# A new order for the prologue of a fused attention and MLP kernel on one core

## The chip, the cores and the metric

The kernel runs on one core of one Trainium2 chip. The metric is the device time of one execution in microseconds (us). Executions of one and the same kernel spread here by more than the effect under study: the kernel before took between 1108.5 and 1114.3 us in the rounds below. So small differences are read in two ways: from times taken in alternating rounds on one chip, with a 95% interval, and from the trace of one execution of each kernel, which shows where in that run each microsecond was spent. e1 to e4 ran on one chip, e5 to e8 on a second, e9 to e12 on a third.

PE is the matmul engine and PEld its weight loads, DVE the vector engine, ACT the scalar engine, POOL the general engine, and SP the engine that issues most DMAs (483 of the 485 in the profile before).

## The reference, cut to what matters

```python
x  = A_x                                  # 2048 tokens x 1024, bf16
xn = layernorm(x)
s  = attention(xn, wqkv, wo)              # 32 heads of 32
g  = silu(gelu(layernorm(xn) @ w1 + b1) @ w2 + b2)      # 3584 hidden
return x + s * g
```

The token tiles (16 tiles of 128 tokens) must be normed and transposed before anything else can run.

## The kernel before

A small list scheduler in the kernel's Python fixes the order of instructions on every engine. The program lets engines wait for each other only by semaphores. The run is cut into "units": a unit has the scores of two key tiles for one group of four heads (`s_unit`, PE), their exp (`exp_unit`, two ACT instructions) and the product with V (`pv_unit`, PE). There are 512 units. Units 0 to 7 are the prologue, which also norms and transposes the tokens and makes K, Q and V of the first heads. From unit 8 on, PE does one "dense" item in each unit (an MLP or projection piece), as the string `PLAN` lists them; that is over 1,000 us of the run.

```python
def norm_pair(p):                        # two token tiles at a time
    more = p + 1 < NP
    if more and p >= 2: stat(2 * p + 2)  # bn_stats, bn_aggr on DVE
    nbias(p)
    xnorm(2 * p); xnorm(2 * p + 1)       # DVE, into one of 4 buffers
    if more:
        if p < 2: stat(2 * p + 2)
        stat(2 * p + 3)
        rstd(p + 1)                      # DVE add, POOL pow
    ycoef(p)                             # POOL

stat(0); stat(1); rstd(0); norm_pair(0); transp_pair(0)

def pro_unit(p):
    if p + 1 < NP: norm_pair(p + 1)
    if p < 3: ynorm(p)
    if 0 < p < NP - 1: transp_pair(p + 1)    # PE transposes, ACT copies to xnT
    pair_kq(p)                               # K and Q: 64 matmuls; two ACT copies
    pair_v(p)                                # V: 64 matmuls; one ACT copy
    if p == 0: transp_pair(1)
# ...
while u < NU + LAG or ...:
    if u < NP: pro_unit(u)
    if u == 4: load_y(0)
    if 4 <= u < NP: load_sub(0, u - 4)       # first MLP weights, 256 KB each
    s_unit(u); exp_unit(u); pv_unit(u - 1)
    if u >= NP: ...                          # one dense item of PLAN
```

The biases `b1` and `b2` are loaded at the start by POOL, as two DMAs of single elements (4,640 packets for 0.02 MB on the page).

The softmax here doesn't subtract the row's maximum and nothing guards it: scores larger than these inputs give would overflow.

Of the kernel before, what the change touches and what calls it, by code (L numbers as in the profile page):

```python
# [13 lines left out]
a v a a a q a q a v a v a a a q a a v a q a a v q a a v a a q a q a a v q a q a a a q q v a a q w3 w4 w3 w4 v w4 w2 w2 w2 a a v a q v v a q q a a a a a q a q a a q a a v a q a q q a a a v v a a a q v a a a a q q a a w3 v w3 w4 w4 w4 q v q v w2 v q w3 w3 a a a v v q a a a q a a q q a a a q q a v a q a v a a q a q a a a a v a a q a q v v v a a q q q v a q q a w3 q v q w5 q w4 w3 q w3 w4 w2 w4 a a a v v a a q a a q a q q v a a q a q v a q a a a a q a a a q a a v a a a a v a v a q a v q q w3 w4 v q w4 w4 w4 v w4 w3 w4 a a a q q a a a a v a v a a a a a v q a a v a a a q a a a v a a q q v a q q a a q a q q q a v w3 v w4 w4 q w4 w4 w4 w4 w4 a a a a q q a a q a a q a a a q a q q a a a a a a a a a a q q a a a a a q a q w2 w4 w3 w4 w2 w3 w5 o o o o o o o o o o o o w4 o o o o o o o o o o o o o o o o o o o o o o o o o o o . o o o o o o o . o o  # L14
# [153 lines left out]
def bass_recurrent_scan__mha_block__mixer_channel_mlp__prompt_kernel(  # L168
# [42 lines left out]
    with ExitStack() as st:  # L211
# [42 lines left out]
        xnb = [hflat[:, i * D:(i + 1) * D] for i in range(4)]  # L254
# [28 lines left out]
        for tb in range(4):  # L283
            load_x(tb)
            if tb in (1, 3):
                load_wq(0, (1 if tb == 1 else 0,))
        load_x(4)
        load_x(5)
        load_wq(0, (2,))
        for tb in range(6, NT):  # L290
            load_x(tb)
# [4 lines left out]
        op("gpsimd", lambda e: e.dma_start(b1T[:], B_b1.rearrange("(fb p) -> p fb", p=128)), w=["b1"], dma="b1", c=256)  # L296
        op("gpsimd", lambda e: e.dma_start(b2h[:], B_b2.rearrange("(nb p) -> p nb", p=128)), w=["b2"], dma="b2", c=64)

# [9 lines left out]
        def rstd(b):  # L308
            lo, hi = 2 * b, 2 * b + 2
            L = lambda k: lnp[:, k, lo:hi]  # L310
            mvk = [("mv", t) for t in range(lo, hi)]
            op("vector", lambda e: e.tensor_scalar_add(L(0), mv[:, lo:hi, 1], EPS), r=mvk, w=[("l0", b)], c=169.0)
            op("gpsimd", lambda e: e.tensor_tensor(L(2), L(0), mhalf[:, 0:2], op=ALU.pow), r=[("l0", b), "mhalf"], w=[("l2", b)], c=708.0)  # L313

        def nbias(b):
            lo, hi = 2 * b, 2 * b + 2
            L = lambda k: lnp[:, k, lo:hi]
            mvk = [("mv", t) for t in range(lo, hi)]
            op("vector", lambda e: e.scalar_tensor_tensor(L(3), mv[:, lo:hi, 0], -1.0, L(2), op0=ALU.mult, op1=ALU.mult),
               r=mvk + [("l2", b)], w=[("l3", b)], c=107.0)  # L320

        def ycoef(b):
            lo, hi = 2 * b, 2 * b + 2
            L = lambda k: lnp[:, k, lo:hi]
            mvk = [("mv", t) for t in range(lo, hi)]
            op("gpsimd", lambda e: e.tensor_tensor(L(4), mv[:, lo:hi, 1], L(2), op=ALU.mult), r=mvk + [("l2", b)], w=[("l4", b)])
            op("gpsimd", lambda e: e.tensor_tensor(L(4), L(4), L(2), op=ALU.mult), r=[("l4", b), ("l2", b)], w=[("l4", b)])
            op("gpsimd", lambda e: e.tensor_scalar(L(4), L(4), 1.0, EPS, op0=ALU.mult, op1=ALU.add), r=[("l4", b)], w=[("l4", b)])
            op("gpsimd", lambda e: e.tensor_tensor(L(5), L(4), mhalf[:, 0:2], op=ALU.pow), r=[("l4", b), "mhalf"], w=[("l5", b)], c=760.0)
            op("gpsimd", lambda e: e.tensor_tensor(L(6), L(2), L(5), op=ALU.mult), r=[("l5", b), ("l2", b)], w=[("l6", b)])  # L330
            op("gpsimd", lambda e: e.tensor_tensor(L(7), L(3), L(5), op=ALU.mult), r=[("l5", b), ("l3", b)], w=[("l7", b)])

        def xnorm(tb):
            i = tb % 4
            op("vector", lambda e: e.tensor_scalar(xnb[i], xst[:, tb * D:(tb + 1) * D], lnp[:, 2, tb:tb + 1], lnp[:, 3, tb:tb + 1],  # L335
                                                   op0=ALU.mult, op1=ALU.add),
               r=[("xst", tb), ("l2", tb // 2), ("l3", tb // 2)], w=[("xnb", i)], c=545.0)
# [7 lines left out]
        pro_banks = [4, 5, 7]  # L345
        pbk = {"n": 0}
# [5 lines left out]
        def transp(tb):  # L352
            i, bk = tb % 4, pro_bank()
# [129 lines left out]
        def w1_item(c, f):  # L483
# [14 lines left out]
            def fin(bk):  # L498
# [30 lines left out]
                def gate(i, xq, kq, fq):  # L529
                    op("vector", lambda e: e.scalar_tensor_tensor(hT[:, fq, 0:n], ut[:, i, 0:n], 1.0, xq[:, 0:n], op0=ALU.add, op1=ALU.mult),  # L530
                       r=[kus[i], kq], w=[("hT", fq)] + ([("xnb", i) for i in range(4)] if c == 0 else []), c=151 + 1.042 * n)
                    busy.difference_update((kq, kus[i]))
                    have.add((c, fq))
# [92 lines left out]
        def pair_kq(p):  # L626
            t0, bk = 256 * p, pro_bank()

            def f(e):
                for which, off in ((1, 0), (0, 256)):  # L630
# [3 lines left out]
                return ins  # L634
            op("tensor", f, r=[("wq", 0), ("wq", 1), ("xnT", 2 * p), ("xnT", 2 * p + 1)], w=[("b", bk)], c=("col", 16, 256))
            for nm, dst, off in (("KT", KT, 0), ("QT", QT, 256)):
                op("scalar", lambda e, dst=dst, off=off: e.activation(dst[0][:, t0:t0 + 256], bank(bk, off, off + 256), ACT.Copy),
                   r=[("b", bk)], w=[(nm, 0, 2 * p), (nm, 0, 2 * p + 1)], c=263.0)
# [14 lines left out]

        def norm_pair(p):

            more = p + 1 < NP
            if more and p >= 2:
                stat(2 * p + 2)
            nbias(p)
            xnorm(2 * p)  # L660
            xnorm(2 * p + 1)
            if more:
                if p < 2:
                    stat(2 * p + 2)
                stat(2 * p + 3)
                rstd(p + 1)
            ycoef(p)

        def transp_pair(p):
            transp(2 * p)  # L670
            transp(2 * p + 1)

        stat(0)
        stat(1)
        rstd(0)
        norm_pair(0)
        transp_pair(0)

        def pro_unit(p):
            if p + 1 < NP:  # L680
                norm_pair(p + 1)
            if p < 3:
                ynorm(p)
            if 0 < p < NP - 1:
                transp_pair(p + 1)
            pair_kq(p)
            pair_v(p)
            if p == 0:
                transp_pair(1)


# [12 lines left out]
        DU = NP  # L704
# [136 lines left out]
        while u < NU + LAG or state["qi"] < total or dq or act_tasks:  # L841
# [5 lines left out]
            if u == 4:  # L847
                load_y(0)
            if 4 <= u < NP:
                load_sub(0, u - 4)  # L850
# [3 lines left out]
            if u < NU:  # L854
                exp_unit(u)
            if LAG <= u < NP:
                pv_unit(u - LAG)
            if u >= NP and state["qi"] < total:
                qi = state["qi"]
                entry = flat[qi]  # L860
                state["qi"] += 1
                if entry:
                    it, lo, hi = entry
                    for hp, which in loads.pop(qi, ()):
                        if hp < HG // 2:
                            load_wq(hp, which)
# [77 lines left out]
```

## Time and profile before

| | before |
|---|---|
| time, median of the first 3 runs | 1110.45 us |
| span of the profiled run | 1108.7 us |
| first transpose on PE | 8.15 us |
| scores of unit 1, 3, 8 start | 24.87, 35.84, 59.28 us |

The start of the scores of unit 8 is the hand-over from the prologue to the dense part.

The windows view of the kernel before gives each engine's busy time in stretches of the run; the first column is the stretch and the second its length.

```profile
core 0: us, PE busy (x) PEld busy (x) DVE busy (x) ACT busy (x) POOL busy (x), PEclk, DMA share, GB/s
0.00:25.00 25.00, 13.95 (x320) 10.87 (x320) 19.64 (x49) 10.59 (x15) 11.89 (x30) 1.00 1.13 254
25.00:57.00 32.00, 32.00 (x1000) 27.23 (x992) 14.88 (x39) 27.36 (x41) 12.10 (x34) 1.00 0.27 68
60.00:1050.00 990.00, 980.41 (x27104) 631.53 (x27100) 559.00 (x1250) 968.12 (x1098) 0.00 (x0) 1.00 0.40 115
```

PE is idle for 11 us of the first 25 and for nothing from 25 to 57. In the dense part PE and ACT are both nearly full.

The chain of waits of the kernel before, in order of time (start, us, what):

```profile
19.18 1.08 PE ps L357 x16
20.26 1.26 PE ps L366 x37
21.52 0.62 issue
22.14 2.79 PE ps L366 x91
24.93 0.33 PE ps L761 x8
...
56.79 0.60 ACT VP L651
57.39 1.84 ACT P L773 x2
59.23 0.05 issue
59.28 0.40 PE ps L761 x8
```

L357 are the transposes, L366 all projections, L761 the scores.

The DMA view of the kernel before over the first 14 us (packets, MB, share of the 16 engines):

```profile
q1 hardware_dynamic: 3787, 3.05, 83.3%
q0 software_dynamic: 3659, 0.01, 40.6%
```

The second line is the biases.

### The profile page before, as it was taken

To read this page: it belongs to the slowest core of one execution; us is meant where nothing else is said; L and a number is where in the kernel's file an instruction comes from. 1 tells how busy PE (TensorE), PEld (TensorE's weight loads), DVE (VectorE), ACT (ScalarE), POOL (GpSimd) and SP (SyncE) were. 2 spreads that over 40 slices of the span, in tenths; PEclk is the share of its full clock that TensorE was granted. 3 is DMA by queue.
4 is the path that set the end of the run, shared out by engine and by line. 5 is a ranking of instruction groups with operands and counts; after the bars stand their busy time and mean duration, and the time that the engine had idled before them with its cause. 6 is when DMAs were issued, how large, how long until landed. Compare 5 with 4: busy or idle time off the path is not lost.

```text
span 1108.7 us, 63340 instructions
## 1 busy us (share of the span) xinstructions
PE 1082.7 (98%) x29952; PEld 706.5 (64%) x29952; DVE 630.4 (57%) x1415; ACT 1049.5 (95%) x1197; POOL 24.0 (2%) x64
## 2 busy tenths in 40 slices
PE   6999999999999999999999999999999999999998
PEld 4866666666666666666666666666666666666665
DVE  8468762377742477652276852277743377624556
ACT  4899999899999999999999999999999999999994
POOL 4300000000000000000000000000000000000000
PEclk9999999999999999999999999999999999999999
DMA  9245255323353323333433334433234324557353
GB/s 237 71 145 174 89 146 153 114 79 108 99 150 98 89 80 114 110 87 88 130 108 92 115 76 126 144 111 108 80 104 118 111 81 144 159 155 156 96 136 108
DMA packets 202420, 129.93 MB, mean 117 GB/s; under 512 B 45488, under 2 KB 192944, under 8 KB 202160
## 3 DMA queue, kind: packets, MB, share of 16 engines
q1 hardware_dynamic: 197520, 125.86, 39.7%
q8 instruction: 234, 3.83, 1.4%
q0 software_dynamic: 4640, 0.02, 0.6%
q14 instruction: 26, 0.21, 0.1%
HBM read 104.87 MB, written 12.58 MB: 106 GB/s over the span
## 4 chain that ended last, share of the span: by engine, by line
PE 65%; ACT 32%; DVE 2%; issue 1%; DMA 0%; POOL 0%
PE ps L366 41%; ACT P L773 29%; PE ps L761 10%; PE ps L790 7%; PE ps L793 7%; ACT u L524 3%; DVE stats L303 1%; PE ps L357 1%; ACT thz L566 0%; DMA OT<-in_A_x_dram 0%; DVE hT L335 0%; DVE wq L614 0%; POOL lnp L313 0%; DVE mv L305 0%; DVE xb L507 0%
## 5 line engine op out<-in xcount | busy, mean ns | idle before, releaser
L773 ACT ACTIVATE P<-ps 128x1024 bf16<-128x1024 f32 x1024 | 970.0, 1069 | 18.1 <-PE ps L761 11.9
L793 PE MATMUL ps<-P,ones 128*32 128x256 bf16 x4096 | 257.7, 273 | 0.6 <-issue 0.5
L790 PE MATMUL ps<-P,VP 128*32 128x256 bf16 x4096 | 257.5, 273 | 0.0
L366 PE MATMUL ps<-hT,war 128*32 128x352 bf16 (+1 forms) x5376 | 226.1, 309 | 1.5 <-issue 1.4
L366 PE MATMUL ps<-yTc,war 128*32 128x352 bf16 (+1 forms) x5376 | 226.4, 309 | 0.4 <-issue 0.4
L761 PE MATMUL ps<-QT,KT 32*128 32x256 bf16 x4096 | 204.1, 273 | 7.6 <-ACT P L773 5.5
L366 PEld LDWEIGHTS ps<-hT,war 128*32 128x32 bf16 x5376 | 128.0, 96 | 76.2 <-issue 27.6
L366 PEld LDWEIGHTS ps<-yTc,war 128*32 128x32 bf16 x5376 | 127.5, 96 | 75.8 <-DVE xb L507 17.2
L562 DVE TENSOR_SCALAR zh<-ps,b2h 128x352 f32<-128x352 f32 (+1 forms) x48 | 27.5, 573 | 207.4 <-PE ps L366 207.4
L507 DVE TENSOR_SCALAR xb<-ps,b1T 128x352 f32<-128x352 f32 (+1 forms) x168 | 96.2, 573 | 78.5 <-PE ps L366 75.3
L761 PEld LDWEIGHTS ps<-QT,KT 32*128 32x128 bf16 x4096 | 61.0, 92 | 119.8 <-issue 65.7
L366 PE MATMUL ps<-xnT,wq 128*32 128x352 bf16 (+2 forms) x3200 | 130.0, 306 | 2.1 <-DMA wq<-in_A_wqkv_dram 1.5
L790 PEld LDWEIGHTS ps<-P,VP 128*32 128x32 bf16 x4096 | 110.4, 97 | 21.4 <-issue 1.7
L793 PEld LDWEIGHTS ps<-P,ones 128*32 128x32 bf16 x4096 | 110.5, 97 | 19.6 <-issue 1.1
L530 DVE SCALAR_TENSOR_TENSOR hT<-u,xb 128x352 bf16<-128x352 f32 (+1 forms) x168 | 83.8, 508 | 62.3 <-ACT u L524 62.2
L366 PEld LDWEIGHTS ps<-xnT,wq 128*32 128x32 bf16 x3200 | 77.5, 97 | 41.6 <-DVE xb L507 10.7
L517 DVE SCALAR_TENSOR_TENSOR u<-u,xb 128x352 f32<-128x352 f32 (+1 forms) x168 | 82.5, 509 | 1.9
L513 DVE TENSOR_TENSOR u<-xb 128x352 f32<-128x352 f32 (+1 forms) x168 | 82.5, 508 | 0.8
L524 ACT ACTIVATE u<-u 128x704 f32<-128x704 f32 (+1 forms) x84 | 69.9, 833 | 0.0
L366 PE MATMUL ps<-wq,xnT 128*32 128x256 bf16 x2048 | 66.6, 274 | 1.8 <-issue 1.1
L366 PE MATMUL ps<-xnT,OT 128*32 128x352 bf16 (+1 forms) x1536 | 62.9, 309 | 0.2 <-DVE wq L614 0.2
L366 PEld LDWEIGHTS ps<-wq,xnT 128*32 128x32 bf16 x2048 | 50.2, 96 | 14.0 <-DVE xb L507 5.5
(44 smaller groups left out, 435.5 us busy)
## 6 DMA issues: line engine op xcount, KB each, us to landing
war<-in_B_w_dram SPq DMA_DIRECT2D x336, 256.0 KB, 3.9
wq<-in_A_wqkv_dram SPq DMA_DIRECT2D x12, 512.0 KB, 5.3
OT<-in_A_x_dram SPq DMA_DIRECT2D x16, 256.0 KB, 7.7
y_scratch<-OT SPq DMA_DIRECT2D x16, 256.0 KB, 2.9
xnT<-in_A_x_dram SPq DMA_DIRECT2D x16, 256.0 KB, 3.8
out_dram<-wq SPq DMA_DIRECT2D x16, 256.0 KB, 2.0
gT_scratch<-gst SPq DMA_DIRECT2D x40, 88.0 KB, 1.7
xnT<-in_A_wo_dram SPq DMA_DIRECT2D x1, 2048.0 KB, 9.2
```

The source lines that it names most:

```text
L303: op("vector", lambda e, c=c: e.bn_stats(stats[:, tb, c, :], xt[:, c * 512:(c + 1) * 512]), r=[("xst", tb)], w=[("st", tb, c)], c=677.0)
L366: ins = e.matmul(outs(j), lhsT=lhs(j), rhs=rhs, start=start, stop=stop, tile_position=(0, 32 * j), skip_group_check=True)
L507: x0 = op("vector", lambda e: e.tensor_scalar(xb[:, 0:n], bank(bk, 0, n), b1T[:, f:f + 1], None, op0=ALU.add), r=[("b", bk), "b1"], w=[kx] ...
L513: x = op("vector", lambda e: e.tensor_tensor(ub[:, 0:n], xb[:, 0:n], xb[:, 0:n], op=ALU.mult), r=[kx], w=[ku], c=151 + 1.042 * n)
L517: x = op("vector", lambda e: e.scalar_tensor_tensor(ub[:, 0:n], ub[:, 0:n], 1.0 / 0.044715, xb[:, 0:n], op0=ALU.add, op1=ALU.mult), r=[kx, ...
L524: x = op("scalar", lambda e: e.activation(ut[:, :, 0:n], ut[:, :, 0:n], ACT.Tanh, scale=0.7978845608028654 * 0.044715), r=kus, w=kus, c=48 ...
L530: op("vector", lambda e: e.scalar_tensor_tensor(hT[:, fq, 0:n], ut[:, i, 0:n], 1.0, xq[:, 0:n], op0=ALU.add, op1=ALU.mult), r=[kus[i], kq] ...
L562: x0 = op("vector", lambda e: e.tensor_scalar(zh[:, 0:n], bank(bk, 0, n), 0.25, b2h[:, nb:nb + 1], op0=ALU.mult, op1=ALU.add), r=[("b", bk ...
L761: ins = e.matmul(bank(bks[j], kh * 256, (kh + 1) * 256), lhsT=KT[i2][32 * j:32 * j + 32, k0:k0 + 128], rhs=QT[i2][32 * j:32 * j + 32, qb * ...
L773: op("scalar", lambda e, p=p, sl=sl: e.activation(pb[:, 2 * p:2 * p + 2, :, :].rearrange("p a b q -> p (a b q)"), ps[:, sl * 1024:(sl + 1) ...
L790: e.matmul(bankq(ACC, j, 0, QW), lhsT=VP[vp][:, kb, vo + 32 * j:vo + 32 * j + 32], rhs=pb[:, j, kh, :], start=first, stop=False, tile_posi ...
L793: ins = e.matmul(bankq(ACC, j, QW, 2 * QW), lhsT=ones[:, 0:32], rhs=pb[:, j, kh, :], start=False, stop=last, tile_position=(0, 32 * j), sk ...
```

## The change

The intent was a shorter start: let PE begin sooner, keep DVE ahead of it, and leave the DMA engines to what is needed first. The diff, cut to its core:

```diff
 PLAN = """
-a v a a a q ...
+. a v a a a q ...                    # a leading empty entry
-xnb = [... for i in range(4)]
+xnb = [... for i in range(9)]        # nine norm buffers
-# loads: x0 x1 wqK x2 x3 wqQ x4 x5 wqV x6 ... x15, then b1, b2
+# loads: x0 x1 wqK x2 x3 wqQ wqV x4 ... x11; x12 to x15 in units 0 and 1
+def load_bias(): ...                 # reads ("xst", NT - 1): after the last token tile
 def norm_pair(p):
+    if p == 0:
+        stat(0); rstd(0, 1); stat(1); rstd(1, 2)
+        for t in (0, 1): nbias(t, t + 1); xnorm(t)
+        stat(2); stat(3); rstd(2, 4)
     ...
-stat(0) ... norm_pair(0); transp_pair(0)
+for p in range(1 + AHEAD): norm_pair(p)          # AHEAD = 2
+transp(0); transp(1)
 def pro_unit(p):
+    if 2 <= p < 5: ynorm(p - 2)
+    for t in range(12 + 2 * p, min(14 + 2 * p, NT)): load_x(t)
+    norm_pair(p + 3)
+    if p == 4: load_bias()
+    if p == 1: load_sub(0, 0..3)                 # first MLP weights, was units 4 to 7
+    if TLATE < p: transp(2 * p + 2), transp(2 * p + 3)        # TLATE = 2
     pair_kq(p)                                   # K and Q as two steps with own waits
+    if p == 0: transp(2), transp(3)
     pair_v(p)
+    if 1 <= p <= TLATE: transp(2 * p + 2), transp(2 * p + 3)
-DU = NP
+DU = NP - 1                                      # the plan starts at unit 7
```

In units 1 and 2 the transposes of the next pair now come after V instead of before K and Q. The diff also contains paths that are never taken with its settings (norms on ACT, transposes by DMA).

More of the change, by code (lines that the diff above doesn't have):

```diff
@@ L13 @@
 PLAN = """
-a v a a a q a q a v a v a a a q a a v a q a a v q a a v a a q a q a a v q a q a a a q q v a a q w3 w4 w3 w4 v w4 w2 w2 w2 a a v a q v v a q q a a a a a q a q a a q a a v a q a q q a a a v v a a a q v a a a a q q a a w3 v w3 w4 w4 w4 q v q v w2 v q w3 w3 a a a v v q a a a q a a q q a a a q q a v a q a v a a q a q a a a a v a a q a q v v v a a q q q v a q q a w3 q v q w5 q w4 w3 q w3 w4 w2 w4 a a a v v a a q a a q a q q v a a q a q v a q a a a a q a a a q a a v a a a a v a v a q a v q q w3 w4 v q w4 w4 w4 v w4 w3 w4 a a a q q a a a a v a v a a a a a v q a a v a a a q a a a v a a q q v a q q a a q a q q q a v w3 v w4 w4 q w4 w4 w4 w4 w4 a a a a q q a a q a a q a a a q a q q a a a a a a a a a a q q a a a a a q a q w2 w4 w3 w4 w2 w3 w5 o o o o o o o o o o o o w4 o o o o o o o o o o o o o o o o o o o o o o o o o o o . o o o o o o o . o o
+. a v a a a q a q a v a v a a a q a a v a q a a v q a a v a a q a q a a v q a q a a a q q v a a q w3 w4 w3 w4 v w4 w2 w2 w2 a a v a q v v a q q a a a a a q a q a a q a a v a q a q q a a a v v a a a q v a a a a q q a a w3 v w3 w4 w4 w4 q v q v w2 v q w3 w3 a a a v v q a a a q a a q q a a a q q a v a q a v a a q a q a a a a v a a q a q v v v a a q q q v a q q a w3 q v q w5 q w4 w3 q w3 w4 w2 w4 a a a v v a a q a a q a q q v a a q a q v a q a a a a q a a a q a a v a a a a v a v a q a v q q w3 w4 v q w4 w4 w4 v w4 w3 w4 a a a q q a a a a v a v a a a a a v q a a v a a a q a a a v a a q q v a q q a a q a q q q a v w3 v w4 w4 q w4 w4 w4 w4 w4 a a a a q q a a q a a q a a a q a q q a a a a a a a a a a q q a a a a a q a q w2 w4 w3 w4 w2 w3 w5 o o o o o o o o o o o o w4 o o o o o o o o o o o o o o o o o o o o o o o o o o o . o o o o o o o . o o
 """
@@ L253, in bass_recurrent_scan__mha_block__mixer_channel_mlp__prompt_kernel @@
         hflat = hT[:].rearrange("p k t -> p (k t)")
-        xnb = [hflat[:, i * D:(i + 1) * D] for i in range(4)]
+        NXN = 9
+        xnb = [hflat[:, i * D:(i + 1) * D] for i in range(NXN)]
         xst = OT[:].rearrange("p g s -> p (g s)")
@@ L281, in load_wq @@
                 op("sync", lambda e, src=src, t3=t3: e.dma_start(wq[:, t3, :, :], src), w=[("wq", t3)], dma=f"wq{t3}", c=512)
-        for tb in range(4):
-            load_x(tb)
-            if tb in (1, 3):
-                load_wq(0, (1 if tb == 1 else 0,))
-        load_x(4)
-        load_x(5)
-        load_wq(0, (2,))
-        for tb in range(6, NT):
+        XUP = 12
+        load_x(0)
+        load_x(1)
+        load_wq(0, (1,))
+        load_x(2)
+        load_x(3)
+        load_wq(0, (0, 2))
+        for tb in range(4, XUP):
             load_x(tb)
@@ L295, in bass_recurrent_scan__mha_block__mixer_channel_mlp__prompt_kernel, with load_bias @@
         op("vector", lambda e: e.memset(ones[:], 1.0), w=["ones"])
-        op("gpsimd", lambda e: e.dma_start(b1T[:], B_b1.rearrange("(fb p) -> p fb", p=128)), w=["b1"], dma="b1", c=256)
-        op("gpsimd", lambda e: e.dma_start(b2h[:], B_b2.rearrange("(nb p) -> p nb", p=128)), w=["b2"], dma="b2", c=64)
+        def load_bias():
+            op("gpsimd", lambda e: e.dma_start(b1T[:], B_b1.rearrange("(fb p) -> p fb", p=128)), r=[("xst", NT - 1)], w=["b1"], dma="b1", c=256)
+            op("gpsimd", lambda e: e.dma_start(b2h[:], B_b2.rearrange("(nb p) -> p nb", p=128)), r=[("xst", NT - 1)], w=["b2"], dma="b2", c=64)
         def stat(tb):
@@ L306, in stat, with rstd, nbias @@
                r=[("st", tb, 0), ("st", tb, 1)], w=[("mv", tb)], c=209.0)
-        def rstd(b):
-            lo, hi = 2 * b, 2 * b + 2
+        def rstd(lo, hi):
             L = lambda k: lnp[:, k, lo:hi]
-            mvk = [("mv", t) for t in range(lo, hi)]
-            op("vector", lambda e: e.tensor_scalar_add(L(0), mv[:, lo:hi, 1], EPS), r=mvk, w=[("l0", b)], c=169.0)
-            op("gpsimd", lambda e: e.tensor_tensor(L(2), L(0), mhalf[:, 0:2], op=ALU.pow), r=[("l0", b), "mhalf"], w=[("l2", b)], c=708.0)
-        def nbias(b):
-            lo, hi = 2 * b, 2 * b + 2
+            op("vector", lambda e: e.tensor_scalar_add(L(0), mv[:, lo:hi, 1], EPS), r=[("mv", t) for t in range(lo, hi)],
+               w=[("l0", t) for t in range(lo, hi)], c=169.0)
+            op("gpsimd", lambda e: e.tensor_tensor(L(2), L(0), mhalf[:, 0:hi - lo], op=ALU.pow), r=[("l0", t) for t in range(lo, hi)] + ["mhalf"],
+               w=[("l2", t) for t in range(lo, hi)], c=708.0)
+        def nbias(lo, hi):
             L = lambda k: lnp[:, k, lo:hi]
-            mvk = [("mv", t) for t in range(lo, hi)]
             op("vector", lambda e: e.scalar_tensor_tensor(L(3), mv[:, lo:hi, 0], -1.0, L(2), op0=ALU.mult, op1=ALU.mult),
-               r=mvk + [("l2", b)], w=[("l3", b)], c=107.0)
+               r=[("mv", t) for t in range(lo, hi)] + [("l2", t) for t in range(lo, hi)], w=[("l3", t) for t in range(lo, hi)], c=107.0)
         def ycoef(b):
@@ L324, in ycoef @@
             L = lambda k: lnp[:, k, lo:hi]
+            l2k = [("l2", t) for t in range(lo, hi)]
             mvk = [("mv", t) for t in range(lo, hi)]
-            op("gpsimd", lambda e: e.tensor_tensor(L(4), mv[:, lo:hi, 1], L(2), op=ALU.mult), r=mvk + [("l2", b)], w=[("l4", b)])
-            op("gpsimd", lambda e: e.tensor_tensor(L(4), L(4), L(2), op=ALU.mult), r=[("l4", b), ("l2", b)], w=[("l4", b)])
+            op("gpsimd", lambda e: e.tensor_tensor(L(4), mv[:, lo:hi, 1], L(2), op=ALU.mult), r=mvk + l2k, w=[("l4", b)])
@@ L328, in ycoef @@
+            op("gpsimd", lambda e: e.tensor_tensor(L(4), L(4), L(2), op=ALU.mult), r=[("l4", b)] + l2k, w=[("l4", b)])
             op("gpsimd", lambda e: e.tensor_scalar(L(4), L(4), 1.0, EPS, op0=ALU.mult, op1=ALU.add), r=[("l4", b)], w=[("l4", b)])
             op("gpsimd", lambda e: e.tensor_tensor(L(5), L(4), mhalf[:, 0:2], op=ALU.pow), r=[("l4", b), "mhalf"], w=[("l5", b)], c=760.0)
-            op("gpsimd", lambda e: e.tensor_tensor(L(6), L(2), L(5), op=ALU.mult), r=[("l5", b), ("l2", b)], w=[("l6", b)])
@@ L331, in ycoef @@
-            op("gpsimd", lambda e: e.tensor_tensor(L(7), L(3), L(5), op=ALU.mult), r=[("l5", b), ("l3", b)], w=[("l7", b)])
-        def xnorm(tb):
-            i = tb % 4
-            op("vector", lambda e: e.tensor_scalar(xnb[i], xst[:, tb * D:(tb + 1) * D], lnp[:, 2, tb:tb + 1], lnp[:, 3, tb:tb + 1],
-                                                   op0=ALU.mult, op1=ALU.add),
-               r=[("xst", tb), ("l2", tb // 2), ("l3", tb // 2)], w=[("xnb", i)], c=545.0)
+            op("gpsimd", lambda e: e.tensor_tensor(L(6), L(2), L(5), op=ALU.mult), r=[("l5", b)] + l2k, w=[("l6", b)])
@@ new lines, in ycoef, with xnorm @@
+            op("gpsimd", lambda e: e.tensor_tensor(L(7), L(3), L(5), op=ALU.mult), r=[("l5", b)] + [("l3", t) for t in range(lo, hi)], w=[("l7", b)])
+        def xnorm(tb, eng="vector"):
+            i = tb % NXN
+            rk = [("xst", tb), ("l2", tb), ("l3", tb)]
+            if eng == "vector":
+                op("vector", lambda e: e.tensor_scalar(xnb[i], xst[:, tb * D:(tb + 1) * D], lnp[:, 2, tb:tb + 1], lnp[:, 3, tb:tb + 1],
+                                                       op0=ALU.mult, op1=ALU.add), r=rk, w=[("xnb", i)], c=545.0)
+            else:
+                op("scalar", lambda e: e.activation(xnb[i], xst[:, tb * D:(tb + 1) * D], ACT.Identity, bias=lnp[:, 3, tb:tb + 1],
+                                                    scale=lnp[:, 2, tb:tb + 1]), r=rk, w=[("xnb", i)], c=903.0)
@@ L345, in bass_recurrent_scan__mha_block__mixer_channel_mlp__prompt_kernel @@
         pro_banks = [4, 5, 7]
+        TDMA = 16
         pbk = {"n": 0}
@@ L352, in transp @@
         def transp(tb):
-            i, bk = tb % 4, pro_bank()
+            i = tb % NXN
+            if tb >= TDMA:
+                op("sync", lambda e: e.dma_start_transpose(xnT[:, :, tb * 128:(tb + 1) * 128], xnb[i]),
+                   r=[("xnb", i)], w=[("xnT", tb)], dma=f"xt{tb % 4}", c=256)
+                return
+            bk = pro_bank()
             def f(e):
@@ L530, in gate @@
                     op("vector", lambda e: e.scalar_tensor_tensor(hT[:, fq, 0:n], ut[:, i, 0:n], 1.0, xq[:, 0:n], op0=ALU.add, op1=ALU.mult),
-                       r=[kus[i], kq], w=[("hT", fq)] + ([("xnb", i) for i in range(4)] if c == 0 else []), c=151 + 1.042 * n)
+                       r=[kus[i], kq], w=[("hT", fq)] + ([("xnb", i) for i in range(NXN)] if c == 0 else []), c=151 + 1.042 * n)
                     busy.difference_update((kq, kus[i]))
@@ L627, in pair_kq, with f @@
             t0, bk = 256 * p, pro_bank()
-            def f(e):
-                for which, off in ((1, 0), (0, 256)):
+            for which, nm, dst, off in ((1, "KT", KT, 0), (0, "QT", QT, 256)):
+                def f(e, which=which, off=off):
                     for dc in range(DC):
@@ L633, in f @@
                                   xnT[:, dc, t0:t0 + 256], dc == 0, dc == DC - 1)
-                return ins
-            op("tensor", f, r=[("wq", 0), ("wq", 1), ("xnT", 2 * p), ("xnT", 2 * p + 1)], w=[("b", bk)], c=("col", 16, 256))
+                    return ins
+                op("tensor", f, r=[("wq", which), ("xnT", 2 * p), ("xnT", 2 * p + 1)], w=[("b", bk, off)] + ([("b", bk)] if off == 0 else []), c=("col", 8, 256))
             for nm, dst, off in (("KT", KT, 0), ("QT", QT, 256)):
                 op("scalar", lambda e, dst=dst, off=off: e.activation(dst[0][:, t0:t0 + 256], bank(bk, off, off + 256), ACT.Copy),
-                   r=[("b", bk)], w=[(nm, 0, 2 * p), (nm, 0, 2 * p + 1)], c=263.0)
+                   r=[("b", bk), ("b", bk, 256)], w=[(nm, 0, 2 * p), (nm, 0, 2 * p + 1)], c=263.0)
         def pair_v(p):
@@ L652, in pair_v @@
                r=[("b", bk)], w=[("VP", 0, 2 * p), ("VP", 0, 2 * p + 1)], c=480.0)
+        TLATE = 2
+        ACTN, AHEAD, YLATE = 9, 2, 2
         def norm_pair(p):
-            more = p + 1 < NP
-            if more and p >= 2:
-                stat(2 * p + 2)
-            nbias(p)
-            xnorm(2 * p)
-            xnorm(2 * p + 1)
-            if more:
-                if p < 2:
-                    stat(2 * p + 2)
-                stat(2 * p + 3)
-                rstd(p + 1)
-            ycoef(p)
@@ L669, in transp_pair @@
-        def transp_pair(p):
-            transp(2 * p)
-            transp(2 * p + 1)
-        stat(0)
-        stat(1)
-        rstd(0)
-        norm_pair(0)
-        transp_pair(0)
-        def pro_unit(p):
-            if p + 1 < NP:
-                norm_pair(p + 1)
-            if p < 3:
-                ynorm(p)
-            if 0 < p < NP - 1:
-                transp_pair(p + 1)
+            lo, hi = 2 * p, 2 * p + 2
+            if p == 0:
+                stat(0)
+                rstd(0, 1)
+                stat(1)
+                rstd(1, 2)
+                for t in (0, 1):
+                    nbias(t, t + 1)
+                    xnorm(t)
+                stat(2)
+                stat(3)
+                rstd(2, 4)
+            else:
+                if 1 < p < NP - 1:
+                    stat(hi)
+                nbias(lo, hi)
+                xnorm(lo)
+                if p < ACTN:
+                    xnorm(lo + 1)
+                    if lo >= TDMA:
+                        transp(lo)
+                        transp(lo + 1)
+                if p + 1 < NP:
+                    if p == 1:
+                        stat(hi)
+                    stat(hi + 1)
+                    rstd(hi, hi + 2)
@@ new lines, in norm_pair, with norm_act @@
+            ycoef(p)
+        def norm_act(p):
+            if p >= ACTN:
+                transp(2 * p)
+                xnorm(2 * p + 1, "scalar")
+                transp(2 * p + 1)
+        for p in range(1 + AHEAD):
+            norm_pair(p)
+        transp(0)
+        transp(1)
+        def pro_unit(p):
+            if YLATE <= p < YLATE + 3:
+                ynorm(p - YLATE)
+            for t in range(XUP + 2 * p, min(XUP + 2 * p + 2, NT)):
+                load_x(t)
+            if p + 1 + AHEAD < NP:
+                norm_pair(p + 1 + AHEAD)
+            if p == 4:
+                load_bias()
+            if p == 1:
+                for q in range(4):
+                    load_sub(0, q)
+            if TLATE < p and 2 * p + 2 < TDMA:
+                transp(2 * p + 2)
+                transp(2 * p + 3)
@@ L686, in pro_unit, with pro_late @@
             pair_kq(p)
+            if p == 0:
+                transp(2)
+                transp(3)
             pair_v(p)
-            if p == 0:
-                transp_pair(1)
+            if 1 <= p <= TLATE:
+                transp(2 * p + 2)
+                transp(2 * p + 3)
+        def pro_late(p):
+            if p + 1 + AHEAD < NP:
+                norm_act(p + 1 + AHEAD)
         w1s = [w1_item(c, f) for c in range(NCH) for f in range(FB)]
@@ L846, in bass_recurrent_scan__mha_block__mixer_channel_mlp__prompt_kernel @@
                 op("vector", lambda e: e.tensor_scalar_mul(b2h[:], b2h[:], 0.5), r=["b2"], w=["b2"])
-            if u == 4:
+            if u == 5:
                 load_y(0)
-            if 4 <= u < NP:
-                load_sub(0, u - 4)
             if u < NU:
@@ L855, in bass_recurrent_scan__mha_block__mixer_channel_mlp__prompt_kernel @@
                 exp_unit(u)
+            if u < NP:
+                pro_late(u)
             if LAG <= u < NP:
                 pv_unit(u - LAG)
-            if u >= NP and state["qi"] < total:
+            if u >= NP - 1 and state["qi"] < total:
                 qi = state["qi"]
@@ L861, in bass_recurrent_scan__mha_block__mixer_channel_mlp__prompt_kernel @@
                 state["qi"] += 1
+                for hp, which in loads.pop(qi, ()):
+                    if hp < HG // 2:
+                        load_wq(hp, which)
                 if entry:
                     it, lo, hi = entry
-                    for hp, which in loads.pop(qi, ()):
-                        if hp < HG // 2:
-                            load_wq(hp, which)
                     if lo == 0:
```

## The prediction

> **What bounds the kernel now.** The windows view splits the run in two. From 60 to 1050 us PE is busy 99% and ACT 98%; this dense part (attention interleaved with MLP and projections) is limited by both, and the change leaves its order of work alone. Only the first 57 us (eight units of norm, transpose, K/Q/V, first scores) is rearranged. There the chain of waits runs: first tiles landing at 3.36; DVE statistics and norms until 19.13; then PE almost without a gap until V of unit 7 ends at 56.77. PE is idle about 11 us of the first 25, 8.15 of them before its first transpose. From unit 2 a unit costs PE 5.49 us (chain) and ACT about 5.2 (timeline: exp 1.94, two transpose copies 1.95, K/Q 0.72, V 0.60). A second gap, 1.66 us before the scores of unit 8 (waits view), waits for VP copy 0.60 plus exp 1.94.
>
> **"One unit sooner" is nominal.** The plan gains a leading empty entry and starts at unit 7 instead of 8, so every dense item keeps its unit; the 1.66 us gap stays.
>
> **Costed steps**, with the timeline's durations:
> 1. Tile 0's own rstd and norm: before, the pow on POOL starts at 6.59, after both tiles' statistics. After: tile 0's pow runs under tile 1's statistics (1.45 us), its norm about 6.9 to 7.4, first transpose about 7.5 instead of 8.15; the second norm ends near 8.3. Both copies (0.97 each) end about 10.5 instead of 11.16. Gain about 0.7.
> 2. Biases late: 4,640 packets for 0.02 MB, 40% of the DMA engines' time in the first 14 us (DMA view), while traffic ran 207 to 306 GB/s against 353 to 378 at 16 to 20 us. [...] Their going, with K split from Q, removes the 1.46 us wait for K/Q weights (about 0.25 beyond the copies) and the 0.64 for V weights. K of unit 0 starts about 10.6 instead of 11.50.
> 3. It stays cold: the first 64 matmuls took 3.61 us against 1.93 later. [...] the change doesn't avoid it.
> 4. Statistics ahead and nine norm buffers take DVE off the chain, but ACT then leads: in units 2 and 3 PE should wait 0.5 to 1 us for transpose copies queued behind exp. Transposes of tiles 8 and 9 near 30 to 30.5 instead of 31.23.
>
> From there both run at 5.49 per unit, so V of unit 7 ends about 55.6 instead of 56.77, and the dense part shifts with it: about 1.1 us saved of 1110.45. Late biases should land before the first bias add at 61.03.
>
> **Predicted: 1109.2 us, 8 in 10 between 1106.5 and 1111.0.** Chances: faster by over 2% 0.01, within 2% 0.98, slower 0.01.
>
> **Right if:** first transpose near 7.5; no DMA wait of PE in the prologue; PE waits on ACT copies between 20 and 35; V of unit 7 ends 55 to 56.3; PE and ACT busy in the rest unchanged; the gap before unit 8 still about 1.7.
>
> **Wrong if:** tiles 4 and 5, now behind the V weights, land after about 13.4 and hold DVE; the early MLP weight loads crowd the token tiles; the biases land after 58 and stop the bias adds; or the list scheduler, fed other start clocks, interleaves DVE and ACT otherwise in the dense part (a microsecond or two either way).

The waits of step 2 (1.46 and 0.64 us) and the 3.61 us of step 3 are measured, and the sum is: V of unit 7 at 55.6 instead of 56.77, 1.17 us, which the text rounds to "about 1.1". "Cold" in step 3 stands for no more than those slow first matmuls: the granted clock was 1.00 there too (the windows view from 10 to 15 us), so why they are slow is not shown.

## More of the kernel before

Transposes, K/Q and V rotate through three PSUM banks (the tile `ps`, which the matmuls write in the traces), so V of a unit can also wait for the ACT copy of an earlier transpose (0.62 us in e7).

The piece "issue" of 0.62 us at 21.52 stands in the middle of K and Q of unit 1: PE waits there for nothing that the profile can name.

## The result, and the profile after

| | before | after |
|---|---|---|
| median, 4 runs each | 1110.88 us | 1111.84 us |
| lowest to highest | 1109.95 to 1112.0 | 1110.14 to 1113.06 |
| ratio, 95% interval | | 1.0007, 0.9989 to 1.0025 |
| scores of unit 1, 3, 8 start | 24.87, 35.84, 59.28 | 24.37, 36.90, 60.59 |

The ratio is the mean time of one kernel's fast runs over that of the other's of the same rounds, so it is not quite the ratio of the medians. By it the two kernels are the same. The predicted gain of 1.1 us is not there, and the median lies outside the predicted range. The trace says more: the prologue became 1.31 us longer.

The chain of waits of the changed kernel from the first K on:

```profile
10.65 3.60 PE ps L376 x49
14.26 1.52 PE ps L367 x16
15.77 1.86 PE ps L376 x64
...
17.96 1.63 PE ps L376 x54
19.60 1.59 issue
21.19 2.27 PE ps L376 x74
...
23.48 0.60 ACT VP L660
24.07 1.90 ACT xnT L370 x2
...
34.06 0.93 ACT xnT L370
...
35.03 1.93 PE ps L376 x64
...
58.70 1.84 ACT P L815 x2
...
60.59 0.40 PE ps L803 x8
```

Up to 19.60 nothing looks wrong. K of unit 0 starts at 10.65, and K of unit 1 starts at 17.89 by the timeline, against 20.25 before: PE is 2.4 us ahead. Then the "issue" piece is 1.59 us instead of 0.62. After it ACT leads the chain twice (L370, the copies out of the transposes), and PE waits.

The waits of PE in the first 62 us, first before, then after (who waited for whom, us in total, times, longest):

```profile
PE ps L366 <- DMA wq<-in_A_wqkv_dram: 2.1, 2, 1.5
PE ps L761 <- ACT P L773: 1.7, 1, 1.7
PE ps L366 <- issue: 0.6, 1, 0.6
```

```profile
PE ps L376 <- ACT xnT L370: 2.6, 3, 1.3
PE ps L803 <- ACT P L815: 1.6, 1, 1.6
PE ps L376 <- issue: 1.6, 1, 1.6
```

The wait for weights has gone and ACT has taken its place. The first of its three waits (1.27) only precedes K of unit 0; the other two, 0.70 and 0.59, come in units 2 and 3.

The windows view of the changed kernel:

```profile
0.00:25.00 25.00, 14.64 (x332) 12.10 (x336) 19.62 (x50) 10.43 (x15) 9.43 (x29) 1.00 0.84 274
25.00:57.00 32.00, 30.71 (x948) 26.03 (x944) 15.42 (x40) 27.67 (x41) 15.02 (x36) 1.00 0.56 52
60.00:1050.00 990.00, 979.71 (x27124) 632.34 (x27128) 558.89 (x1251) 968.81 (x1099) 0.00 (x0) 1.00 0.40 116
```

PE gained 0.69 us of work in the first 25 us and lost 1.29 in the next 32. The rest is as it was. A comparison of the two instruction streams shows that the order on PE, DVE and ACT in the dense part is identical (but for neighbouring matmuls that start almost together), so a shift there can only come from the start or from chance.

**What the 1.59 us is.** The trace also records single DMA packets. One queue, which the profile calls "q8 instruction", carries 234 packets of 16,384 bytes in each of these runs. PE has 29,952 matmuls and as many weight loads, and 59,904 / 234 is 256. That it is 256 exactly is partly chance, since PE has other instructions too (151 or 152 semaphore instructions). But from the start of one packet to the next PE starts 255.2 to 255.6 matmuls and weight loads on average, in each of the 14 traces (255.3 in those before and after, by a straight line through all packets). So I take these packets for PE's instructions, about 256 to a packet; the expectations call such a packet a "refill", and so do I below. In the kernel before, PE stopped after its 221st recorded matmul and 222nd weight load; after the change it stopped after its 222nd and 223rd, though the order of work up to there is another. So it is a place in the instruction stream, and not a place in the computation. In both it went on about 1.2 us after the first packet of that queue had landed (1.21 to 1.36 us in the six profiles with such a gap):

```text
                      PE stops   packet starts  takes   PE goes on
before                 21.52        19.92        0.96     22.14
after                  19.60        18.88        1.08     21.19
```

PE arrived 1.92 us sooner, the packet landed only 0.92 sooner.

### The profile page after: what moved, and what is told of

Its sections match the earlier page's. It is cut to its first block, busy times and chain, and to the rows that moved or that the text cites. A ratio compares the mean times of both kernels' runs of the same rounds, so it can differ in the third digit from the quotient of the medians.

```text
span 1108.3 us, 63341 instructions
## 1 busy us (share of the span) xinstructions
PE 1081.7 (98%) x29952; PEld 707.5 (64%) x29952; DVE 630.5 (57%) x1417; ACT 1049.5 (95%) x1197; POOL 24.4 (2%) x65
## 4 chain that ended last, share of the span: by engine, by line
PE 61%; ACT 37%; DVE 1%; issue 1%; DMA 0%
PE ps L376 39%; ACT P L815 33%; PE ps L803 10%; PE ps L832 6%; PE ps L835 6%; ACT u L534 3%; ACT xnT L370 1%; PE ps L367 1%; ACT thz L576 0%; DMA OT<-in_A_x_dram 0%; DVE stats L304 0%; ACT VP L660 0%; DVE wq L624 0%; DVE xb L517 0%; DVE wq L626 0%
## 5 line engine op out<-in xcount | busy, mean ns | idle before, releaser
L803 PEld LDWEIGHTS ps<-QT,KT 32*128 32x128 bf16 x4096 | 60.9, 92 | 120.4 <-issue 65.1
L376 PEld LDWEIGHTS ps<-xnT,wq 128*32 128x32 bf16 x3200 | 77.8, 97 | 42.9 <-DVE xb L517 10.5
```

The source lines that it names most:

```text
L376: ins = e.matmul(outs(j), lhsT=lhs(j), rhs=rhs, start=start, stop=stop, tile_position=(0, 32 * j), skip_group_check=True)
L803: ins = e.matmul(bank(bks[j], kh * 256, (kh + 1) * 256), lhsT=KT[i2][32 * j:32 * j + 32, k0:k0 + 128], rhs=QT[i2][32 * j:32 * j + 32, qb * ...
```

## The experiments

The theories, as the expectations below name them:

- **A**: PE loses the time at 20 us because the packet with its next instructions queues behind bulk DMA traffic. The changed kernel issues 1 MB of MLP weights at 15.68 to 17.66 us, right into that moment.
- **B** (rival): the refill takes a fixed time from the instruction that asks for it, whatever the DMA engines do.
- **C**: ACT is the second limit: the copies out of the transposes stand in its queue just ahead of the exp, and PE waits for them.

All of them gave correct results. The edits are against the changed kernel unless said otherwise.

### e1: the MLP weight loads late again

```diff
-            if p == 1:
-                for q in range(4): load_sub(0, q)
+            if 4 <= u < NP: load_sub(0, u - 4)        # in the main loop, as before
```

> The changed kernel with the four first MLP weight loads (1 MB) put back to units 4 to 7. Theory A (PE loses its time at about 20 us because its second 16,384-byte instruction refill queues behind bulk DMA traffic): the instruction packet starts earlier than 18.88 and PE's gap in K of unit 1 shrinks from 1.59 us to 1.3 or less, V of unit 7 ends before 57.8 instead of 58.08. Only part of the gain, since token tiles still fill the DMA engines until about 18. Theory B (the refill takes a fixed time from the instruction that asks for it, whatever the DMA engines do): gap stays 1.5 to 1.7 and V of unit 7 ends at 58.0 to 58.2.

The packet at 18.88 is the first of its queue in the trace of the changed kernel; that it is PE's "second" is not shown.

The packet starts at 16.82 instead of 18.88, and the gap is not smaller but gone. The timeline of PE in this run shows K and then V of unit 1 without a break (start, busy, engine, line, op, tiles, forms, count; an idle time before would stand in brackets):

```profile
18.00 1.93 PE L376 MATMUL ps<-xnT,wq 128*32 128x256 bf16 x64
19.75 1.92 PE L376 MATMUL ps<-wq,xnT 128*32 128x256 bf16 x64
```

In the changed kernel the first of these lines falls into two, of 54 and of 10 matmuls, with 1.59 us of "issue" between them.

Scores of unit 8 start at 58.56 instead of 60.59. The instruction streams of PE are the same, so B is wrong. V of unit 7 ends at 56.06. The start does not explain this: scores of unit 0 began at 17.67, in the changed kernel at 17.57. One point the theory leaves open: the DMA view of e1 shows the engines still full until about 18.0, so the packet started among other traffic; 1 MB less was queued, and it came 2.06 us sooner. The time was 1109.77 against 1111.0 before (ratio 0.9989, 0.9964 to 1.0015).

### e2: also the last token tiles really late

```diff
-            for t in range(XUP + 2 * p, min(XUP + 2 * p + 2, NT)):
-                load_x(t)
+            if p == 1:                       # after pair_kq(1)
+                for t in range(XUP, NT):
+                    load_x(t, after=[pg.lists["tensor"][-1]])
```

In the change itself the "late" tiles wait for nothing: SP issues them right behind the others (the last twelve tiles in one piece, from 7.09 to 15.64).

> As the run before, and token tiles 12 to 15 wait for K/Q of unit 1, so that no bulk load is under way from about 17 to 21 us. Theory A: the refill packet starts at about 17 to 17.5 and the gap falls to under 0.4 us; V of unit 7 ends at about 56.5 to 57.0 and the dense part starts that much sooner (about 1.2 us less in the whole time). Theory B: the gap stays at 1.5 to 1.7 us. If the gap goes and V of unit 7 still ends at 58, then the ACT queue (transpose copies placed just ahead of the exp) was the limit and the gap only hid it (theory C).

There is no gap. V of unit 7 ends at about 55.4 (its copy starts at 55.45), scores of unit 8 start at 57.93. That is lower than I expected by theory A, and within 0.2 us of the 55.6 that the prediction had for V of unit 7. Part of this is luck. The first matmuls are slow in these runs (64 of them took 3.60 us in the changed kernel, where 64 later ones took 1.93), and when they become fast differs between executions of one and the same kernel. The transposes of tiles 2 and 3, in the first profile of the changed kernel and in its second (e12):

```profile
14.19 1.58 PE L367 MATMUL ps<-ident,hT 128*128 128x128 bf16 x16
14.03 1.07 PE L367 MATMUL ps<-ident,hT 128*128 128x128 bf16 x16
```

So scores of unit 0 began at 17.57 in the first and at 16.89 in the second. In e2 they began at 16.80: 0.77 of the 2.66 us by which its unit 8 is sooner than in the changed kernel were won before the refill mattered. e1 is the cleaner comparison. The two ACT waits, 0.70 and 0.59, are unchanged. Time 1109.24 against 1111.0, ratio 0.9983 (0.9951 to 1.0014).

### e3: the biases early again

```diff
-            if p == 4: load_bias()
+        op("gpsimd", ... b1T ..., w=["b1"], dma="b1")      # at the start, as before
+        op("gpsimd", ... b2h ..., w=["b2"], dma="b2")
```

> The changed kernel with the two bias loads back at the start. My prediction's step 2 (their 4,640 small packets slow the weights): K of unit 0 starts at 11.2 or later instead of 10.65, waiting for a DMA, and the V weights make PE wait too; S of unit 0 0.5 us later or more. The rival (the packets take engine time but no time of the weights, because K weights come first in this order): K of unit 0 still at 10.6 to 10.8. The refill of about 49 us takes about 1 us again instead of 1.97, since the biases no longer run beside it.

K of unit 0 starts at 10.67, to be compared with 10.65, and no wait for weights appears. The gap in K of unit 1 is there again (1.70). So the late biases did not help here: with the new order of the weight loads, and K split from Q, the weights are in time anyway. Late biases even cost 0.2 us: at 49.27 a refill ran beside them (their packets start from 48.05 to 51.66), took 1.97 us, and PE lost 0.26; in this run the refill at 48.34 took 1.01. Scores of unit 8 start at 60.40. The one execution took 1108.02 us, thanks to a dense part shorter than usual.

### e4: tiles 0 and 1 normed as a pair again

```diff
-                stat(0); rstd(0, 1); stat(1); rstd(1, 2)
-                for t in (0, 1): nbias(t, t + 1); xnorm(t)
+                stat(0); stat(1); rstd(0, 2); nbias(0, 2); xnorm(0); xnorm(1)
```

> The changed kernel with tiles 0 and 1 normed as a pair again. Step 1 of my prediction: first transpose at about 8.1 instead of 7.50 and K of unit 0 at 11.2 instead of 10.65. By theory A that half microsecond does not reach the end of the prologue: PE arrives later at the end of its instructions, the refill comes when it came, the gap is 1.0 to 1.2 instead of 1.59, and V of unit 7 ends within 0.2 us of 58.08. By the rival (each step of the start adds up) V of unit 7 ends at about 58.6.

First transpose 8.43, K of unit 0 11.58: the start is 0.93 us later. Scores of unit 8 start at 60.67 against 60.59. It looks as if the step worked and nothing of it arrived, but this pair of profiles cannot show that. In e4 the matmuls became fast sooner (3.34 us for K and Q of unit 0 and 1.07 for the next transposes, against 3.60 and 1.58), so scores of unit 0 began only 0.14 later (17.71 against 17.57), and PE came to the stop only 0.14 later. Against the second profile of the changed kernel (e12) unit 8 is 0.44 later. The gap, 1.78, was not shorter as I had expected; the packet started later too (19.27). That the refill swallows a lead is seen better in the two profiles of the changed kernel: in e12 PE came to the stop 0.67 us sooner (18.93 against 19.60) and went on only 0.09 sooner (21.10 against 21.19).

### e5: transposes of tiles 6 and 7 ahead of K and Q of unit 2

```diff
 # on top of e2
-        TLATE = 2
+        TLATE = 1
```

> The quiet kernel (late weight loads, tiles 12 to 15 gated) with the transposes of tiles 6 and 7 moved ahead of K/Q of unit 2. Theory C (after the refill wait is gone, what is left of the loss in units 1 to 3 is ACT: the copies out of the transposes are queued behind copies of V and ahead of the exp, so PE waits 0.70 for the copy of tile 5 and 0.59 for the copy of tile 8): one of the two waits goes, scores of unit 3 start at about 33.9 instead of 34.50, scores of unit 8 at about 57.3 instead of 57.93. Rival (the waits only show ACT being full from there on): the waits move, the total stays, unit 8 at 57.9.

Scores of unit 3 start at 33.98, of unit 8 at 57.42. One wait of PE for a copy is left (0.59), the other is gone. Scores of unit 2 to scores of unit 3 take 5.49 us instead of 6.26. Theory C holds, and its rival doesn't. Time 1108.96 against 1111.03, ratio 0.9985 (0.9959 to 1.0011); one of the four runs took 1114.57.

### e6: the first MLP item really in unit 7

```diff
 # on top of e2
-. a v a a a q ...
+a v a a a q ...                     # and the "." at place 249 instead
```

> The quiet kernel with the leading empty entry of the plan moved to place 249, so that the first MLP item really runs in unit 7 and every item up to there one unit sooner. The order on the vector engine changes in the dense part by itself. PE's gap of 1.65 us before the scores of unit 8 falls to about 0.3; scores of unit 8 stay at 57.9 (exp decides that). If PE limits the dense part, the whole time falls by about 1.3 us; if ACT limits it, it stays within 0.3 us.

This failed: 1114.54 against 1111.03, ratio 1.0032 (1.001 to 1.0055). The gap before the scores of unit 8 did fall from 1.65 to 0.46 us. But the next item needs V weights that can be loaded only after V of unit 7 has used the buffer, and PE waited 0.79 us before it. (The waits view puts this down to a DVE instruction that ended at 59.17; the weights, issued at 55.55, landed 3.5 us later, at about the same time. In e8 the same wait, 0.98, is put down to the DMA.) The dense part, from the scores of unit 8 to the start of the last exp, then took 1037.84 us, where the profiles with the old order took 1029.3 to 1034.5. In the waits view PE's waits for exp from unit 7 on rose from 4.8 to 6.3 us and those for "issue" from 2.8 to 3.8 on the projections. The scheduler had also reordered DVE, and I had no run left to tell this from the place of the item.

### e7: the kernel before with late biases only

```diff
 # on top of the kernel before
-        op("gpsimd", ... b1T ...); op("gpsimd", ... b2h ...)
+            if p == 6: load_bias()                     # same load_bias as in the change
```

> The kernel before with only the bias loads moved late (issued after the last token tile has landed). By theory A the packets of the biases also kept the DMA engines full at 20 us, so here the refill comes sooner: PE's gap of 0.62 us in K of unit 1 goes, so does most of the 0.64 wait for V weights; scores of unit 8 at 57.9 to 58.4 instead of 59.28. By the rival (late biases do nothing, as early ones did no harm in the changed kernel): scores of unit 8 at 59.1 to 59.4.

The waits for K/Q and V weights went, with the old order of loads. It gained nothing there: V of unit 0 began at 14.96 instead of 15.74, but still ran slowly (2.74 us instead of 1.93) and ended at the same time. The packet came at 17.65 instead of 19.92, and the "issue" gap in K went too. But PE then waited 0.62 us before V, for an ACT copy out of a transpose; V began at 23.02, against 23.00 in the kernel before: scores of unit 2 at 30.37 against 30.35. In the kernel before, the 0.62 us of waiting for instructions were thus hidden by another wait that lasted as long. Later PE lost time twice (units 3 to 4 and 5 to 6 took 5.73 and 5.79 us instead of 5.49), which I put down to refills beside the biases without testing it, and scores of unit 8 came at 59.85, later than the 59.28 of the kernel before. Ratio 0.9997 (0.9977 to 1.0017). Theory A's account of the packet held, my numbers for the end did not.

### e8: e5 and e6 together

> The quiet kernel with both edits (transposes of tiles 6 and 7 ahead, and the first MLP item in unit 7). If both gains add: scores of unit 8 at 57.3, PE's gap before it under 0.4, and 3 to 4 us (0.3%) under the kernel before, near 1107. If only one holds, 1108 to 1109.

Scores of unit 8 start at 57.51 with a gap of 0.45 before, so both edits do what they should in the prologue. Yet the time is 1112.8 against 1111.03, ratio 1.0009 (0.9992 to 1.0025): the dense part is at the upper edge of what was seen with the old order, or just above it (1034.61), and what the start had won is gone. That profile is of the fastest of the six runs of e8 (1110.49); the other five took 1112.61 to 1113.68, so their dense part was most likely longer still.

### e9 and e10: two parts of the change once more, where the refill no longer decides

Both are e5 with one part undone: e9 with the edit of e4, e10 with that of e3.

> The fixed kernel with tiles 0 and 1 normed as a pair again. In the changed kernel undoing this cost nothing at the end of the prologue (60.67 against 60.59), which I put down to the refill. With the refill out of the way the later start should now arrive: K of unit 0 about 0.9 us later (11.5 against 10.61) and scores of unit 8 at 58.0 to 58.4 instead of 57.42. If unit 8 still starts at 57.2 to 57.6, the single norm is worth nothing, whatever the refill does.

Scores of unit 8 at 58.10, against 57.42 in e5 and 57.22 in its repeat. Scores of unit 0 were later by about as much (17.98 against 17.30 and 17.04), so here the later start arrives in full. (The 0.08 of e4, with which the expectation compares, was in part luck, as said there.)

> The fixed kernel with the biases loaded at the start again. In the changed kernel this did no harm (60.40 against 60.59). If late biases matter only where the DMA engines must be quiet for the refill, here the refill packet starts 1 us or more later than 15.5 and a gap of 0.3 to 1.5 us opens in K of unit 1, with unit 8 at 57.8 to 59. If biases never matter: no gap, unit 8 at 57.2 to 57.6.

The packet starts at 18.56, the gap is 2.25, scores of unit 8 start at 59.41. The direction is that of the theory, the size larger than I had expected. The timeline of PE in this run, from where it goes on:

```profile
21.05 0.51 PE L375 MATMUL ps<-xnT,wq 128*32 128x256 bf16 x10 [2.25 <-issue]
```

Again ten matmuls of this step are left when PE stops, as in the changed kernel. Early biases did no harm in e3 only because the refill was late anyway (a gap of 1.70 there, 1.59 without them).

### e11 and e12: the best kernel and the changed one again, five rounds each

> The kernel of e5_tlate1 once more, with five rounds, to see whether it beats the kernel before. If the shift of the dense part is all there is: scores of unit 8 at 57.2 to 57.6 again, the dense stretch 1029 to 1033 as in all runs with this order, and a mean time 1.5 to 2.5 us (0.15 to 0.25%) under the kernel before, which is about the size of the interval. The rival (the total is decided by chance in the dense part): no difference that the interval separates from 1.

> The changed kernel, unedited, once more, with five rounds and a second profile. If the refill is what set its prologue, the gap in K of unit 1 is there again at 1.3 to 1.8 us, and scores of unit 8 are at 60.3 to 60.8; the mean time is 0 to 2 us above the kernel before, and 2 to 4 us above the fixed kernel of the same rounds. If the gap of the first profile was chance, it is missing or under 1 us and unit 8 comes before 60.

| five rounds | median | ratio to before, 95% interval | gap in K of unit 1 | scores of unit 8 |
|---|---|---|---|---|
| before | 1111.06 | 1 | 0.62 (first profile) | 59.28 (first profile) |
| change, e12 | 1109.62 | 0.9992, 0.9979 to 1.0006 | 2.17 | 60.23 |
| e5 again, e11 | 1106.94 | 0.9968, 0.9955 to 0.9982 | none | 57.22 |

The gap of the changed kernel is no chance: it is there in both profiles. Its total cannot be told from that of the kernel before. The kernel of e5 is faster than the kernel before by 0.32%, and its interval excludes 1, which it did not in the first three rounds (0.9985). The 0.32% are about 3.5 us, more than the 2.06 by which unit 8 is sooner; and e12 has a lower median than the kernel before though its unit 8 is 0.95 later. So one or two microseconds of these totals do not come from the prologue, and the gain of e5 is shown for the whole time, its size only roughly.

The chain of waits of e11, at the place where that of the changed kernel had its 1.59 us:

```profile
17.43 3.69 PE ps L376 x128
...
21.14 0.60 ACT VP L660
21.74 1.89 ACT xnT L370 x2
23.64 1.83 ACT P L813 x2
25.47 0.93 ACT xnT L370
```

K, Q and V of unit 1 are one piece of 128 matmuls. The DMA view says why. From 16 to 20 us, busy tenths of the DMA engines in 40 slices and the two queues, first of the changed kernel, then of e11:

```profile
DMA  9999989998999999989999999989998999999999
q1 hardware_dynamic: 947, 1.53, 102.9%
q8 instruction: 1, 0.02, 1.7%
```

```profile
DMA  5449100000000000000000000000000000000000
q1 hardware_dynamic: 43, 0.07, 4.6%
q8 instruction: 1, 0.02, 1.7%
```

In the first the one instruction packet shares the engines with 1.53 MB and starts at 18.88; in the second it starts at 16.39, just as the other traffic ends. Its own duration is 1.08 and 1.07 us: the loss lies ahead of its start and not in it. In the two profiles of the changed kernel the packet started at 18.83 to 18.88, in the six quiet ones (e2, e5, e6, e8, e9, e11) at 15.31 to 16.57. When it was asked for the traces do not show, so where these 2.3 to 3.6 us are spent stays open.

## Why the prediction was wrong

- **Step 1, single norms: right.** First transpose 7.50 (about 7.5 was said), copies done at 10.52 (10.5), K of unit 0 at 10.65 (10.6).
- **Step 2, late biases: right, but not needed.** The waits for weights went. They also go with early biases and the new order of loads (e3), and with late biases and the old order (e7), so either part of the change is enough.
- **Step 3, first matmuls still slow: right.** The first 64 took 3.60 us. What the prediction did not have: how long they stay slow differs between executions (K and Q of unit 0 3.28 to 3.61 us, the next transposes 1.07 to 1.58), and this alone moved scores of unit 0 by 0.68 us between the two profiles of the changed kernel.
- **Step 4: here it failed.** The prediction said "Transposes of tiles 8 and 9 near 30 to 30.5 instead of 31.23"; they came at 31.51. The term missing from the sum was the wait for instructions in K of unit 1. It stood in the chain of the kernel before as "0.62 issue", and I wrote "PE almost without a gap". It measured 1.59 us in one profile and 2.17 in the other. Where it was removed, V of unit 7 ended at 56.06 (e1) and 55.4 (e2, with some luck), where the prediction had 55.6 and a range of 55 to 56.3; with it, at 58.08. The ACT waits were foreseen, and each was sized about right (0.70 and 0.59, for 0.5 to 1; the text does not say whether it meant each or both together, which is 1.29).
- **The sum "From there both run at 5.49 per unit ... about 1.1 us saved".** PE was 2.36 us ahead when K of unit 1 began, but 1.07 of them because the transposes of tiles 4 and 5 were still to do. Of the other 1.29 the longer refill wait took 0.97 (1.59 less 0.62), which leaves 0.32; at the scores of unit 1 PE was 0.50 ahead (24.37 against 24.87), since those transposes took 1.00 from start to start and V of the kernel before had a further short wait. From scores to scores, units 1 to 2 and 2 to 3 took 6.26 and 6.27 us instead of 5.48 and 5.49, mostly by the ACT waits of 0.70 and 0.59: 1.56 lost. With 0.26 for the refill beside the biases this gives 0.50 - 1.56 - 0.26 = -1.32, and the measured shift of unit 8 is 60.59 - 59.28 = 1.31.
- **"One unit sooner is nominal": right.** The gap before unit 8 was 1.64. Making it real (e6) lost time.
- **The range was too narrow.** The total is the prologue plus a dense part, which took between 1029.3 and 1034.5 us in profiles with one and the same order of instructions. That alone moves the total by several microseconds. In the first comparison the shift of 1.3 us and this spread put the median above the range; in the five rounds of e12 the median, 1109.62, would have been inside. So that the total fell outside the range is partly chance. That the prologue became longer instead of shorter is seen in both profiles of the change (unit 8 at 60.59 and 60.23, against 59.28 in the one of the kernel before). Why the dense part varies was not settled: the profiles show small "issue" waits of PE at varying places in it (2.9 us before, 2.2 after), which would fit late refills, but no run tested that.

## What to carry to other kernels

An "issue" wait in a long straight-line program can be the engine waiting for its own instructions, as the experiments here indicate for 0.62 to 2.25 us of PE; it is worth looking at which matmul it stops, and whether an instruction packet lands just before it goes on (here 1.21 to 1.36 us before). When a change made PE reach that place sooner here (by 1.92 us), the wait grew from 0.62 to 1.59 and swallowed most of the gain, and early prefetch of data was what made it long: with the 1 MB of MLP weights issued late (e1) the packet started at 16.82 instead of 18.88, and the wait was gone. That load was issued at 15.68 to 17.66 and first used at 60.9; here it was better held back until the refill was through. And after any gain at the start, follow it through every unit to the hand-over, for a second engine with little slack can give part of it back (ACT was busy for 27.67 of the 32.00 us from 25 to 57 in the changed kernel, 86%, and still cost PE 0.70 and 0.59). And compare profiles unit by unit from the first one on: two executions of one kernel differed by 0.68 us before the place under study.
